# Three raw buffers for late weights, six for reads of h, reads five steps ahead and splits two, in a chain of attention and two feed-forward layers

## The chip, the cores and the metric

The kernel runs on one core of a Trainium2 chip. The metric is the time on the device in microseconds (us), lower is better; the time of a kernel is the median of several runs.

## The reference

Decay attention over 4 batches of 8 heads (576 positions, 64 wide) gives x, 2304 x 512. A feed-forward layer with Mish follows, then one with a maximum of three products. All arrays are float32.

```python
x = attention(q, k, v, f)                       # 2304 x 512
h = x @ moe_w_in                                # 2304 x 2048
g = h * np.tanh(np.log1p(np.exp(h)))            # Mish
y = g @ moe_w_out                               # 2304 x 512
m = np.maximum(np.maximum(y @ w1, y @ w2), y @ w3)   # 2304 x 768
out = m @ moe2_w_out                            # 2304 x 512
```

## The kernel before

Every product of two float32 arrays is made of three matmuls (`mm3`, L180 to L184): each operand is split into a high part and a low part (`split`, L135 to L143: the high part is a copy to the narrower type, L137 on ACT or L139 on POOL; the low part is the difference, L143 on DVE or POOL), and high by high, high by low and low by high are summed in PSUM.

Weights are read in chunks by `load_f32` (L147). A chunk comes in by a DMA of SP as raw 8-byte numbers (the tile r, named `wr` or `wr1`) and is made float32 in the tile `wt` by five operations of DVE: L160, L161, L164, L167 and L171. L160, L167 and L171 read the raw tile. `load_split` then splits `wt`, for the late weights both halves on POOL.

The work has three stages, which overlap at their edges:

1. Attention and h. PE makes x, and h from it in units of 256 tokens by 256 columns; a copy `he` (L542 on ACT, or on DVE) goes to DRAM, to `h_d`. Near its end `load_w_out` reads moe_w_out in 16 chunks of 128 x 512 (tiles `wo`), one for each unit of h. These use the raw tile `wr` with two buffers.
2. y, from about 490 to 717 us. 72 steps (`todo`) run over 5 blocks of tokens and 16 chunks of the 2048 columns: 64 steps with 512 tokens and 12 matmuls each, then 8 with 256 tokens and 24 matmuls. For a step, `load_g` reads h back from `h_d` (DMA on SP, L631), applies Mish on ACT (L634) and splits the result into gh (ACT, L137) and gl (DVE, L143). It is called three steps ahead of the matmuls, with tiles of four buffers each. At the end of a block four copies `ze` of y (tile pool `zst`, four buffers; two by ACT and two by DVE) go to DRAM, to `z_d`; the first 256 tokens of the first block come back at once and are split by ACT and POOL (`y0`).
3. The maximum of three products and the last product, 717 us to the end.

In stage 2 the weights of stage 3 are loaded too. `load_w2` has 24 chunks of 128 x 384 (tiles `wm`) and then 6 of 128 x 512 (`wo2`), and one chunk is asked for at every second step. These use a raw tile `wr1` of their own with one buffer: the DMA of a chunk cannot start before L171 of the chunk ahead has read it. The converted tile `wt` has two buffers in all of this.

Each engine does its instructions in the order of its own list. The lists come from a scheduler that simulates the program with costs of its own; priorities (`tc.high_priority(AHEAD)` around `load_g`) and buffers coming free in that simulation decide what is put first. So a change of buffer numbers moves instructions on all engines.

Of the kernel before, what the change touches and what calls it, by code (L numbers as in the profile page):

```python
# [9 lines left out]
F32 = mybir.dt.float32  # L10
F32R = mybir.dt.float32r
BF16 = mybir.dt.bfloat16
I32 = mybir.dt.int32
# [18 lines left out]
AHEAD = 3000  # L32
BLK = 256
BLK2 = 512
# [33 lines left out]
def tile_decay_attention__mish_ff__max3_ff(  # L68
# [66 lines left out]
    def split(dst_hi, dst_lo, src, eng_hi, eng_lo):  # L135
        if eng_hi == "act":
            nc.scalar.activation(dst_hi, src, AF.Copy)  # L137
        elif eng_hi == "pool":
            nc.gpsimd.tensor_scalar(dst_hi, src, 1.0, 1.0, op0=ALU.mult, op1=ALU.mult)  # L139
        else:  # L140
            nc.vector.tensor_copy(dst_hi, src)
        eng = nc.gpsimd if eng_lo == "pool" else nc.vector
        eng.tensor_tensor(out=dst_lo, in0=src, in1=dst_hi, op=ALU.subtract)  # L143
# [3 lines left out]
    def load_f32(pool, srcs, bufs=None, abs_eng="dve", raw="wr"):  # L147

        m, n = len(srcs), srcs[0].shape[1]
        t = pool.tile([128, m, n], F32, name="wt", tag="wt", bufs=bufs)  # L150
        r = pool.tile([128, m, n, 2], I32, name=raw, tag=raw, bufs=bufs if raw == "wr" else 1)

        with tc.issue_after(pace[-1].ins) if pace else ExitStack():
            for i, src in enumerate(srcs):
                nc.sync.dma_start(r[:, i].rearrange("p n w -> p (n w)"), src.bitcast(I32))
        lo, hi, ti = r[:, :, :, 0], r[:, :, :, 1], t.bitcast(I32)
        if abs_eng == "act":
            nc.scalar.activation(t, hi.bitcast(F32), AF.Abs)
        else:
            nc.vector.tensor_scalar(ti, hi, 0x7FFFFFFF, None, op0=ALU.bitwise_and)  # L160
        nc.vector.tensor_scalar(  # L161
            t, t, F32_MIN_AS_HIGH_HALF, F32_MAX_AS_HIGH_HALF, op0=ALU.max, op1=ALU.min
        )
        nc.vector.tensor_scalar(  # L164
            ti, ti, 3, 0x3FFFFFF8, op0=ALU.logical_shift_left, op1=ALU.bitwise_and
        )
        nc.vector.scalar_tensor_tensor(  # L167
            out=ti, in0=hi, scalar=-0x40000000, in1=ti,
            op0=ALU.bitwise_and, op1=ALU.bitwise_or,
        )  # L170
        nc.vector.scalar_tensor_tensor(  # L171
            out=ti, in0=lo, scalar=29, in1=ti,
            op0=ALU.logical_shift_right, op1=ALU.bitwise_or,
        )
        return t

    def load_split(pool, dst_hi, dst_lo, srcs, eng_hi, eng_lo, bufs=None, abs_eng="dve", raw="wr"):
        split(dst_hi, dst_lo, load_f32(pool, srcs, bufs, abs_eng, raw), eng_hi, eng_lo)

    def mm3(ps, whl, xhl, start, stop):  # L180
        (wh, wl), (xh, xl) = whl, xhl
        nc.tensor.matmul(ps, wh, xh, start=start, stop=False, skip_group_check=True)  # L182
        nc.tensor.matmul(ps, wh, xl, start=False, stop=False, skip_group_check=True)  # L183
        nc.tensor.matmul(ps, wl, xh, start=False, stop=stop, skip_group_check=True)  # L184
# [5 lines left out]
    wst = sa.enter_context(tc.tile_pool(name="wst", bufs=2))  # L190
# [39 lines left out]
    raw = [ap_.tile([128, 640 if c == "v" else S], F32, name=f"raw{c}") for c in "qkv"]  # L230
# [343 lines left out]
    sb = ExitStack()  # L574
# [1 line left out]
    wo = [wop.tile([128, 2, 2, DM], F32R, name=f"wo{fp}") for fp in range(NFP)]  # L576
    stg2 = sb.enter_context(tc.tile_pool(name="stg2", bufs=2, side="right", reuse_waits="tile"))
    gp_ = sb.enter_context(tc.tile_pool(name="gp", bufs=4, side="right", reuse_waits="tile"))
    zst = sb.enter_context(tc.tile_pool(name="zst", bufs=4, side="right", reuse_waits="tile"))
    yps = sb.enter_context(tc.tile_pool(name="yps", bufs=5, space=PSUM, side="right", reuse_waits="tile"))  # L580

    def load_w_out():
# [23 lines left out]
    def load_w2():  # L606
        for c in range(KD):
            for m in range(3):
                src = (moe2_w1, moe2_w2, moe2_w3)[m][c * 128:(c + 1) * 128, :]
                for d in range(0, DFF2, 384):  # L610
                    ds = slice(d, d + 384)
                    load_split(
                        stg2, wm[m][:, 0, c:c + 1, ds], wm[m][:, 1, c:c + 1, ds], [src[:, ds]],
                        "pool", "pool", raw="wr1",
                    )
                    yield
        for c in range(NF2):
            load_split(
                stg2, wo2[:, 0, c:c + 1, :], wo2[:, 1, c:c + 1, :],
                [moe2_w_out[c * 128:(c + 1) * 128, :]], "pool", "pool", raw="wr1",  # L620
            )
            yield

    def load_g(ib, fp, a):

        g = gp_.tile([128, BLK2], F32, name="g")
        gh = gp_.tile([128, BLK2], F32R, name="gh")
        gl = gp_.tile([128, BLK2], F32R, name="gl")
        n = blocks1[ib][1]
        if n == BLK2:  # L630
            nc.sync.dma_start(g, h_d[ib][fp][:, a, :])  # L631
        else:
            nc.sync.dma_start(g.rearrange("p (a n) -> p a n", a=2), h_d[ib][fp][:])
        nc.scalar.activation(g, g, AF.Mish)  # L634
        split(gh, gl, g, "act", "dve")
        return [(t, (gh[:, i * n:(i + 1) * n], gl[:, i * n:(i + 1) * n])) for i, t in enumerate([a] if n == BLK2 else [0, 1])]

    wgen3 = load_w2()
    todo = [(ib, fp, a) for ib, (_, n) in enumerate(blocks1) for fp in range(NFP) for a in range(n // BLK)]
    with tc.high_priority(AHEAD):  # L640
        ahead = [load_g(*t) for t in todo[:3]]
    for step, (ib, fp, a) in enumerate(todo):
        n = blocks1[ib][1]
        if fp == 0 and a == 0:
            y = [yps.tile([128, n], F32, name=f"y{j}", tag="y") for j in range(KD)]
        parts = ahead.pop(0)
        if step + 3 < len(todo):
            with tc.high_priority(AHEAD):
                ahead.append(load_g(*todo[step + 3]))
        for t, g in parts:  # L650
            final = fp == NFP - 1 and t == 1
            for j in range(KD):
                js = slice(j * 128, (j + 1) * 128)
                mm3(y[j], (wo[fp][:, 0, t, js], wo[fp][:, 1, t, js]), g, fp == 0 and t == 0, final)
        if step % 2:
            next(wgen3, None)
        if final:
            for j in range(KD):
                ze = zst.tile([128, n], F32, name="ze", tag="ze")
                if j % 2:  # L660
                    nc.vector.tensor_copy(ze, y[j])
                    nc.sync.dma_start(z_d[ib][:, j, :], ze)
                else:
                    nc.scalar.activation(ze, y[j], AF.Copy)
                    nc.scalar.dma_start(z_d[ib][:, j, :], ze)
            if ib == 0:
                nc.sync.dma_start(y0[0], z_d[0][:, :, 0:BLK])
                split(y0[1], y0[2], y0[0], "act", "pool")
# [12 lines left out]
    for t0, n in blocks2:  # L681
# [13 lines left out]
        for c2 in range(0, NF2, k2):  # L695
            gp = gps[c2 // k2 % 2]
            g = [gp.tile([128, k2, n], F32, name=f"g{m}") for m in range(3)]
# [52 lines left out]
```

## Time and profile before

| | us |
|---|---|
| median of 3 runs | 1026.43 (1024.89 to 1028.39) |
| profiled execution, its time | 1024.48 |
| its span in the trace | 1022.5 |
| PE busy | 955.2 (93%) |
| DVE busy | 511.9 (50%) |
| ACT busy | 422.0 (41%) |
| POOL busy | 378.3 (37%) |

The span is the profiled execution from its first instruction to its last; its own time has 2.0 us around that. PE is TensorE, DVE VectorE, ACT ScalarE, POOL GpSimd, SP the engine that issues most DMAs. "Busy" counts the time in which an engine has work, so it says nothing on which engine the others wait for; that is read from the waits.

### The profile page before, as it was taken

Reading aid. Unit: us, or ns where it says so; the run is one execution under the profiler, and the core shown is the slowest. Engines: PE = TensorE matmul, PEld = TensorE weight load, DVE = VectorE, ACT = ScalarE, POOL = GpSimd, SP = SyncE. Lnnn points to the kernel's source line nnn. Section 1 sums busy time; section 2 is a strip of 40 time slices with the busy share of each in tenths; the row PEclk is TensorE's granted clock in tenths of the full one; section 3 lists DMA queues with packets and bytes.
Section 4 is the critical chain, followed back from the end, with each engine's and each line's share of the span. In section 5 each row is a group of like instructions: output and inputs, shape, how many; then the busy total and the mean of one; then the engine's idle time right before and its main releaser. Section 6 shows DMA issues by size and latency. Waiting matters only on the chain.

```text
span 1022.5 us, 15879 instructions
## 1 busy us (share of the span) xinstructions
PE 955.2 (93%) x5756; PEld 840.6 (82%) x5756; DVE 511.9 (50%) x1159; ACT 422.0 (41%) x920; POOL 378.3 (37%) x437
## 2 busy tenths in 40 slices
PE   4886799999998999998898999999999999999998
PEld 4675689999998999998776777778988888888886
DVE  4868898656556556479645655653211112011110
ACT  4876667666667565421233434332211211211111
POOL 6756875566447521445423423230111111011110
PEclk9987789999999999999898999999999999999999
DMA  6545646545344412765445554552300100200101
GB/s 151 143 141 161 172 131 207 151 145 159 109 143 131 138 57 89 268 208 187 143 144 177 160 185 149 190 172 75 104 21 1 62 21 1 83 1 2 40 0 42
DMA packets 105294, 119.16 MB, mean 117 GB/s; under 512 B 33856, under 2 KB 77376, under 8 KB 105216
## 3 DMA queue, kind: packets, MB, share of 16 engines
q1 hardware_dynamic: 92288, 103.73, 33.0%
q10 hardware_dynamic: 12928, 14.42, 4.0%
q8 instruction: 45, 0.74, 0.3%
q14 instruction: 33, 0.27, 0.1%
HBM read 85.01 MB, written 33.10 MB: 116 GB/s over the span
## 4 chain that ended last, share of the span: by engine, by line
PE 57%; DMA 18%; DVE 17%; issue 2%; ACT 2%; SPq 2%; POOL 1%; DVEq 0%; ACTq 0%; POOLq 0%
PE g L183 7%; PE g L184 7%; PE g L182 7%; DMA wr<-in_moe_w_dram 7%; DMA wr<-in_moe_w_out_dram 5%; PE h L183 4%; PE h L184 4%; PE h L182 4%; PE av L451 4%; PE sc L363 4%; DVE wt L171 3%; PE pp L438 3%; DVE wt L167 3%; PE o L182 2%; PE o L184 2%; PE o L183 2%
## 5 line engine op out<-in xcount | busy, mean ns | idle before, releaser
L182 PE MATMUL h<-xh,wi 128*128 128x256 f32 x576 | 167.4, 292 | 8.2 <-ACT he L542 6.7
L183 PE MATMUL h<-xl,wi 128*128 128x256 f32 x576 | 167.1, 290 | 1.9 <-POOL xl L143 1.9
L184 PE MATMUL h<-xh,wi 128*128 128x256 f32 x576 | 166.2, 289 | 0.0
L143 POOL TENSOR_TENSOR hl<-mx,hh 128x512 fp32r<-128x512 f32 x27 | 36.5, 1350 | 271.3 <-ACT hh L137 271.3
L182 PE MATMUL g<-yh,wm 128*128 128x512 f32 (+1 forms) x360 | 134.5, 374 | 0.0
L183 PE MATMUL g<-yl,wm 128*128 128x512 f32 (+1 forms) x360 | 134.5, 374 | 0.0
L184 PE MATMUL g<-yh,wm 128*128 128x512 f32 (+1 forms) x360 | 134.5, 374 | 0.0
L183 PE MATMUL y<-gl,wo 128*128 128x512 f32 (+1 forms) x320 | 121.6, 380 | 10.5 <-DVE gl L143 10.5
L182 PE MATMUL y<-gh,wo 128*128 128x512 f32 (+1 forms) x320 | 120.5, 378 | 4.6 <-ACT gh L137 3.4
L182 PEld LDWEIGHTS h<-xh,wi 128*128 128x128 f32 x576 | 111.9, 195 | 9.5 <-ACT he L542 7.0
L184 PE MATMUL y<-gh,wo 128*128 128x512 f32 (+1 forms) x320 | 119.5, 375 | 0.0
L183 PEld LDWEIGHTS h<-xl,wi 128*128 128x128 f32 x576 | 111.9, 194 | 3.2 <-POOL xl L143 2.4
L184 PEld LDWEIGHTS h<-xh,wi 128*128 128x128 f32 x576 | 111.8, 194 | 0.3
L634 ACT ACTIVATE g<-g 128x512 f32<-128x512 f32 x72 | 45.5, 632 | 138.5 <-DMA g<-h_d 128.3
L706 DVE TENSOR_TENSOR mx<-g,mx 128x512 f32<-128x512 f32 x27 | 18.7, 691 | 158.6 <-PE g L184 158.6
L183 PEld LDWEIGHTS y<-gl,wo 128*128 128x128 f32 x320 | 61.8, 193 | 26.5 <-DVE gl L143 17.0
L414 ACT ACTIVATE P<-P,mn 128x128 f32<-128x128 f32 (+3 forms) x128 | 70.9, 556 | 27.3 <-DVE mn L408 26.4
L183 PEld LDWEIGHTS g<-yl,wm 128*128 128x128 f32 x360 | 68.2, 189 | 13.4
L184 PEld LDWEIGHTS g<-yh,wm 128*128 128x128 f32 x360 | 68.2, 189 | 13.2
L182 PEld LDWEIGHTS g<-yh,wm 128*128 128x128 f32 x360 | 68.1, 189 | 13.2
L182 PEld LDWEIGHTS y<-gh,wo 128*128 128x128 f32 x320 | 62.0, 194 | 17.3 <-ACT gh L137 4.9
L438 PE MATMUL pp<-ident,P 128*128 128x128 f32 x320 | 64.4, 303 | 11.9 <-POOL P L388 11.7
(101 smaller groups left out, 1989.9 us busy)
## 6 DMA issues: line engine op xcount, KB each, us to landing
g<-h_d SPq DMA_DIRECT2D x72, 256.0 KB, 3.3
h_d<-he ACTq DMA_DIRECT2D x46, 256.0 KB, 2.9
wr<-in_moe_w_out_dram SPq DMA_DIRECT2D x22, 512.0 KB, 4.0
wr<-in_moe_w_dram SPq DMA_DIRECT2D x24, 384.0 KB, 3.4
cb<-cum_d SPq DMA_DIRECT2D x64, 128.0 KB, 3.4
wr<-in_moe_w_in_dram SPq DMA_DIRECT2D x32, 256.0 KB, 3.3
h_d<-he SPq DMA_DIRECT2D x26, 256.0 KB, 3.2
cb<-cum_d SPq DMA_DIRECT2D x32, 144.0 KB, 3.3
```

The lines of the kernel that those rows point to most:

```text
L143: eng.tensor_tensor(out=dst_lo, in0=src, in1=dst_hi, op=ALU.subtract)
L167: nc.vector.scalar_tensor_tensor(out=ti, in0=hi, scalar=-0x40000000, in1=ti, op0=ALU.bitwise_and, op1=ALU.bitwise_or,)
L171: nc.vector.scalar_tensor_tensor(out=ti, in0=lo, scalar=29, in1=ti, op0=ALU.logical_shift_right, op1=ALU.bitwise_or,)
L182: nc.tensor.matmul(ps, wh, xh, start=start, stop=False, skip_group_check=True)
L183: nc.tensor.matmul(ps, wh, xl, start=False, stop=False, skip_group_check=True)
L184: nc.tensor.matmul(ps, wl, xh, start=False, stop=stop, skip_group_check=True)
L363: nc.tensor.matmul(o, lhs, rhs, start=n == 0, stop=n == len(mms) - 1, skip_group_check=True)
L414: nc.scalar.activation(Pt, Pt, AF.Exp, scale=-1.0, bias=mn[:, col - 1:col], accum_out=sm[:, ci:ci + 1],)
L438: nc.tensor.transpose(pp[:, n * 128:n * 128 + 128], Pt[:, k0:k0 + 128], ident)
L451: nc.tensor.matmul(avp[h][:, off:off + w], vl, T[:, i, c:c + w], start=kt == 0 and i == 0 and not (g == 0 and h == 1), stop=last and i == ...
L634: nc.scalar.activation(g, g, AF.Mish)
L706: nc.vector.tensor_tensor(out=mx, in0=g[1], in1=mx, op=ALU.max)
```

## The change

- All late weights share one raw tile `wr` with three buffers, where moe_w_out had two and the later ones one of their own. The room is the same.
- `load_g` only reads h and applies Mish, into tiles `g` with six buffers (before four), and is called five steps ahead (before three). A new function `split_g` makes gh and gl, with three buffers each (before four), and is called two steps ahead (before three). Six and two times three take the room of three times four.
- `zst` has three buffers, where it had four.

```diff
--- before.py
+++ after.py
@@ -148,7 +148,7 @@
 
         m, n = len(srcs), srcs[0].shape[1]
         t = pool.tile([128, m, n], F32, name="wt", tag="wt", bufs=bufs)
-        r = pool.tile([128, m, n, 2], I32, name=raw, tag=raw, bufs=bufs if raw == "wr" else 1)
+        r = pool.tile([128, m, n, 2], I32, name=raw, tag=raw, bufs=3 if pool is not wst else bufs)
 
         with tc.issue_after(pace[-1].ins) if pace else ExitStack():
             for i, src in enumerate(srcs):
@@ -576,7 +576,7 @@
     wo = [wop.tile([128, 2, 2, DM], F32R, name=f"wo{fp}") for fp in range(NFP)]
     stg2 = sb.enter_context(tc.tile_pool(name="stg2", bufs=2, side="right", reuse_waits="tile"))
     gp_ = sb.enter_context(tc.tile_pool(name="gp", bufs=4, side="right", reuse_waits="tile"))
-    zst = sb.enter_context(tc.tile_pool(name="zst", bufs=4, side="right", reuse_waits="tile"))
+    zst = sb.enter_context(tc.tile_pool(name="zst", bufs=3, side="right", reuse_waits="tile"))
     yps = sb.enter_context(tc.tile_pool(name="yps", bufs=5, space=PSUM, side="right", reuse_waits="tile"))
 
     def load_w_out():
@@ -611,42 +611,48 @@
                     ds = slice(d, d + 384)
                     load_split(
                         stg2, wm[m][:, 0, c:c + 1, ds], wm[m][:, 1, c:c + 1, ds], [src[:, ds]],
-                        "pool", "pool", raw="wr1",
+                        "pool", "pool",
                     )
                     yield
         for c in range(NF2):
             load_split(
                 stg2, wo2[:, 0, c:c + 1, :], wo2[:, 1, c:c + 1, :],
-                [moe2_w_out[c * 128:(c + 1) * 128, :]], "pool", "pool", raw="wr1",
+                [moe2_w_out[c * 128:(c + 1) * 128, :]], "pool", "pool",
             )
             yield
 
     def load_g(ib, fp, a):
 
-        g = gp_.tile([128, BLK2], F32, name="g")
-        gh = gp_.tile([128, BLK2], F32R, name="gh")
-        gl = gp_.tile([128, BLK2], F32R, name="gl")
+        g = gp_.tile([128, BLK2], F32, name="g", bufs=6)
         n = blocks1[ib][1]
         if n == BLK2:
             nc.sync.dma_start(g, h_d[ib][fp][:, a, :])
         else:
             nc.sync.dma_start(g.rearrange("p (a n) -> p a n", a=2), h_d[ib][fp][:])
         nc.scalar.activation(g, g, AF.Mish)
+        return g, n, [a] if n == BLK2 else [0, 1]
+
+    def split_g(g, n, tiles):
+        gh = gp_.tile([128, BLK2], F32R, name="gh", bufs=3)
+        gl = gp_.tile([128, BLK2], F32R, name="gl", bufs=3)
         split(gh, gl, g, "act", "dve")
-        return [(t, (gh[:, i * n:(i + 1) * n], gl[:, i * n:(i + 1) * n])) for i, t in enumerate([a] if n == BLK2 else [0, 1])]
+        return [(t, (gh[:, i * n:(i + 1) * n], gl[:, i * n:(i + 1) * n])) for i, t in enumerate(tiles)]
 
     wgen3 = load_w2()
     todo = [(ib, fp, a) for ib, (_, n) in enumerate(blocks1) for fp in range(NFP) for a in range(n // BLK)]
     with tc.high_priority(AHEAD):
-        ahead = [load_g(*t) for t in todo[:3]]
+        read = [load_g(*t) for t in todo[:5]]
+        ahead = [split_g(*read.pop(0)) for _ in range(2)]
     for step, (ib, fp, a) in enumerate(todo):
         n = blocks1[ib][1]
         if fp == 0 and a == 0:
             y = [yps.tile([128, n], F32, name=f"y{j}", tag="y") for j in range(KD)]
         parts = ahead.pop(0)
-        if step + 3 < len(todo):
-            with tc.high_priority(AHEAD):
-                ahead.append(load_g(*todo[step + 3]))
+        with tc.high_priority(AHEAD):
+            if step + 5 < len(todo):
+                read.append(load_g(*todo[step + 5]))
+            if read:
+                ahead.append(split_g(*read.pop(0)))
         for t, g in parts:
             final = fp == NFP - 1 and t == 1
             for j in range(KD):
```

How the lists of the engines differ, at two places. First DVE, where the chunks of 384 columns are converted beside the steps of y (`wt` is the converted chunk, `wr1` or `wr` the raw one, gl the low part of a step's input). Before:

```order
L160 TENSOR_SCALAR wt_7032<-wr1_7033 128x384
L161 TENSOR_SCALAR wt_7032<-wt_7032 128x384
L164 TENSOR_SCALAR wt_7032<-wt_7032 128x384
L143 TENSOR_TENSOR gl_7015<-g_7013,gh_7014 128x512
L167 SCALAR_TENSOR_TENSOR wt_7032<-wr1_7033,wt_7032 128x384
L171 SCALAR_TENSOR_TENSOR wt_7032<-wr1_7033,wt_7032 128x384
L143 TENSOR_TENSOR gl_7044<-g_7042,gh_7043 128x512
L160 TENSOR_SCALAR wt_7080<-wr1_7081 128x384
L161 TENSOR_SCALAR wt_7080<-wt_7080 128x384
```

With the change:

```order
L160 TENSOR_SCALAR wt_7130<-wr_7131 128x384
L171 SCALAR_TENSOR_TENSOR wt_7082<-wr_7083,wt_7082 128x384
L161 TENSOR_SCALAR wt_7130<-wt_7130 128x384
L164 TENSOR_SCALAR wt_7130<-wt_7130 128x384
L143 TENSOR_TENSOR gl_7019<-g_6948,gh_7018 128x512
L167 SCALAR_TENSOR_TENSOR wt_7130<-wr_7131,wt_7130 128x384
L160 TENSOR_SCALAR wt_7178<-wr_7179 128x384
L171 SCALAR_TENSOR_TENSOR wt_7130<-wr_7131,wt_7130 128x384
L161 TENSOR_SCALAR wt_7178<-wt_7178 128x384
L164 TENSOR_SCALAR wt_7178<-wt_7178 128x384
L143 TENSOR_TENSOR gl_7048<-g_6967,gh_7047 128x512
L167 SCALAR_TENSOR_TENSOR wt_7178<-wr_7179,wt_7178 128x384
```

Before, a chunk's five operations and two gl alternate; with the change there is one gl to a chunk, L160 of the next chunk stands ahead of L171 of the one before it, and L164 is followed at once by a gl.

Second, ACT at the end of h (`he` is the copy of h, its DMA goes to `h_d`; `g` on itself is Mish; gh the high part). Before:

```order
L542 ACTIVATE he_6594<-h_6569 128x512
L545 DMA h_d2048_3_104<-he_6594 128x512
L634 ACTIVATE g_6946<-g_6946 128x512
L542 ACTIVATE he_6632<-h_6607 128x512
L545 DMA h_d2048_4_105<-he_6632 128x512
L542 ACTIVATE he_6670<-h_6645 128x512
L545 DMA h_d2048_5_106<-he_6670 128x512
L542 ACTIVATE he_6708<-h_6683 128x512
L545 DMA h_d2048_6_107<-he_6708 128x512
L542 ACTIVATE he_6746<-h_6721 128x512
L545 DMA h_d2048_7_108<-he_6746 128x512
L137 ACTIVATE gh_6870<-g_6869 128x512
```

With the change:

```order
L542 ACTIVATE he_6594<-h_6569 128x512
L545 DMA h_d2048_3_104<-he_6594 128x512
L542 ACTIVATE he_6632<-h_6607 128x512
L545 DMA h_d2048_4_105<-he_6632 128x512
L542 ACTIVATE he_6670<-h_6645 128x512
L545 DMA h_d2048_5_106<-he_6670 128x512
L542 ACTIVATE he_6708<-h_6683 128x512
L137 ACTIVATE gh_6874<-g_6804 128x512
L545 DMA h_d2048_6_107<-he_6708 128x512
L542 ACTIVATE he_6746<-h_6721 128x512
L545 DMA h_d2048_7_108<-he_6746 128x512
L632 ACTIVATE g_6948<-g_6948 128x512
```

The Mish of g_6946 stood ahead of the last four copies of h; the one that answers to it now, g_6948, stands behind the last of them.

## Rows read from the trace of the kernel before

**Rows 1.** The page, part 1: engines over the whole span.
```profile
PE 955.2 (93%) x5756; PEld 840.6 (82%) x5756; DVE 511.9 (50%) x1159; ACT 422.0 (41%) x920; POOL 378.3 (37%) x437
```

**Rows 2.** Busy time by stretch: us from:to, length, each engine, clock, DMA share, GB/s.
```profile
440.00:497.00 57.00, 50.25 (x386) 49.35 (x385) 49.77 (x66) 10.64 (x18) 29.07 (x27) 0.94 0.57 190
497.00:717.00 220.00, 204.83 (x951) 166.78 (x950) 119.07 (x227) 80.02 (x140) 64.19 (x63) 0.97 0.47 153
```

**Rows 3.** Groups of PE by form, 497 to 717 us: busy, mean ns, idle before.
```profile
L183 PE MATMUL y<-gl,wo 128*128 128x512 f32 x247 | 99.3, 402 | 8.3 <-DVE gl L143 8.3
L182 PE MATMUL y<-gh,wo 128*128 128x512 f32 x246 | 97.8, 399 | 3.6 <-ACT gh L137 3.1 <-DVE ze L661 0.5
```

**Rows 4.** Timeline of PE: ten 512-wide starts, then ten 256-wide ones.
```profile
599.54 0.39 PE L183 MATMUL y<-gl,wo 128*128 128x512 f32 x1
...
601.80 0.39 PE L184 MATMUL y<-gh,wo 128*128 128x512 f32 x1
...
707.79 0.28 PE L184 MATMUL y<-gh,wo 128*128 128x256 f32 x1
...
709.00 0.28 PE L182 MATMUL y<-gh,wo 128*128 128x256 f32 x1
```

**Rows 5.** Waits of DVE, 440 to 717 us: us in total, times, longest.
```profile
DVE wt L160 <- DMA wr<-in_moe_w_dram: 57.0, 22, 4.1
...
DVE wt L160 <- POOL wo L143: 2.0, 1, 2.0
```

**Rows 6.** Timeline of DVE: one late chunk of 384 columns and the next one's start.
```profile
510.51 0.36 DVE L160 TENSOR_SCALAR wt<-wr 128x384 int32<-128x384 int32 x1 [3.10 <-DMA wr<-in_moe_w_dram]
...
513.24 0.68 DVE L143 TENSOR_TENSOR gl<-g,gh 128x512 fp32r<-128x512 f32 x1
517.21 0.36 DVE L160 TENSOR_SCALAR wt<-wr 128x384 int32<-128x384 int32 x1 [3.29 <-DMA wr<-in_moe_w_dram]
```

**Rows 7.** Timeline of DVE: one late chunk of 512 columns.
```profile
661.48 0.43 DVE L160 TENSOR_SCALAR wt<-wr 128x512 int32<-128x512 int32 x1 [0.61 <-DMA wr<-in_moe_w_out_dram]
...
663.48 0.69 DVE L143 TENSOR_TENSOR gl<-g,gh 128x512 fp32r<-128x512 f32 x1
664.08 0.69 DVE L171 SCALAR_TENSOR_TENSOR wt<-wr,wt 128x512 int32<-128x512 int32 x1
```

**Rows 8.** Timeline of DVE during the chunks of moe_w_out.
```profile
430.58 1.67 DVE L171 SCALAR_TENSOR_TENSOR wt<-wr,wt 128x512 int32<-128x512 int32 x1
...
464.47 0.51 DVE L160 TENSOR_SCALAR wt<-wr 128x512 int32<-128x512 int32 x1 [0.48 <-DMA wr<-in_moe_w_out_dram]
...
473.45 1.40 DVE L164 TENSOR_SCALAR wt<-wt 128x512 int32<-128x512 int32 x1
...
476.47 0.81 DVE L160 TENSOR_SCALAR wt<-wr 128x512 int32<-128x512 int32 x1 [0.18 <-DMA wr<-in_moe_w_out_dram]
...
489.46 0.54 DVE L160 TENSOR_SCALAR wt<-wr 128x512 int32<-128x512 int32 x1 [0.44 <-DMA wr<-in_moe_w_out_dram]
...
493.85 0.47 DVE L160 TENSOR_SCALAR wt<-wr 128x512 int32<-128x512 int32 x1 [0.51 <-DMA wr<-in_moe_w_out_dram]
```

**Rows 9.** Timeline of POOL: splits of x, of wo, and one of wm.
```profile
439.55 2.72 POOL L143 TENSOR_TENSOR xl<-xr,xh 128x1024 fp32r<-128x1024 f32 x1
...
472.40 0.73 POOL L139 TENSOR_SCALAR wo<-wt 128x512 fp32r<-128x512 f32 x1 [1.82 <-DVE wt L171]
473.21 1.34 POOL L143 TENSOR_TENSOR wo<-wt,wo 128x512 fp32r<-128x512 f32 x1
...
501.70 1.02 POOL L143 TENSOR_TENSOR wm<-wt,wm 128x384 fp32r<-128x384 f32 x1
```

**Rows 10.** Timeline of PE, then of ACT, at the long stall.
```profile
488.45 0.58 PE L182 MATMUL h<-xh,wi 128*128 128x256 f32 x1 [6.75 <-ACT he L542]
...
487.29 0.63 ACT L634 ACTIVATE g<-g 128x512 f32<-128x512 f32 x1 [11.14 <-DMA g<-h_d]
```

**Rows 11.** The page, part 6: reads of h, KB each, us to landing.
```profile
g<-h_d SPq DMA_DIRECT2D x72, 256.0 KB, 3.3
```

## Prediction

> **What bounds the kernel now.** I began with the page's share of busy time [rows 1]: PE 93%, DVE 50%. That says that only TensorE can be worth much, and not where. So next came busy time by stretch [rows 2]. In the stretch 497 to 717 us, where y is made, PE is busy 204.8 of 220 us at a granted clock of 0.97, the higher of its two levels; DVE works 119.1 us and the DMAs carry 153 GB/s at a share of 0.47. Everything after 717 us is the third stage, which the change touches only at its start.
>
> Busy time hides some loss, because pipelined matmuls overlap. The pitch is the better measure [rows 4]: ten 512-wide matmuls start in 601.80 − 599.54 = 2.26 us, so 0.227 us each and 12 × 0.227 = 2.72 us for a step; ten 256-wide ones take 1.22 us, 0.121 us each. The stretch holds some 740 of the first kind (247 and 246 in the forms of [rows 3], and as many of the third product), 192 of the second, and 12 of stage 3: 168 + 23.2 + 1.5 = 193. So PE loses **about 27 us** of 220. What it waits for is gl on DVE, 8.3 us, and gh on ACT, 3.1 us [rows 3]; the rest are stretched starts around these waits.
>
> Why gl is late is seen in DVE's waits [rows 5]: 22 times L160, the first operation of a late chunk, stood for its raw DMA, 57.0 us in all, and every gl behind it stood too. One such chunk is shown whole [rows 6]: L160 waits 3.10 us, the chunk's first three operations and a gl follow, then the next L160 waits 3.29 us. With one raw buffer the transfer cannot start before the last conversion of the chunk ahead has read it. Before the stretch there is one more loss: PE stands 6.75 us for ACT's copy of h, because ACT's Mish ahead of it waited 11.14 us for its read [rows 10]. The most the change can give is 27 + 6.75 = **34 us**.
>
> **What the change does, by part.** *Three raw buffers.* Raw DMAs are issued two chunks earlier, so the 57.0 us of waits should go. But what follows is not an idle DVE. The order (shown above) puts a chunk to **each** gl where there was one to two. All 30 chunks then end by the gl of step 38, where before they ran to step 68; after it 33 gl stand alone. The work isn't smaller, it is moved forward and packed.
>
> *What a packed chunk costs.* Alone, a 384 chunk with a gl takes 513.24 − 510.51 = 2.73 us [rows 6], which is just PE's step of 2.72. A 512 chunk with a gl takes 664.08 + 0.69 − 661.48 = 3.29 us, with the gl 0.60 of it (664.08 − 663.48) [rows 7]; so 2.13 and 2.69 without a gl. Packed, POOL's splits of the chunk ahead lie on it. The trace shows that for the 16 chunks of moe_w_out [rows 8]: L164 takes 1.40 us at 473.45 where POOL's L143 ran 1.34 us from 473.21 [rows 9]. Between 464.47 and 493.85 seven chunks and one gl ran, so (29.38 − 0.60 − 0.18 − 0.44 − 0.51) / 7 = 3.95 us per chunk. Thus POOL's work adds 3.95 − 2.69 = 1.26 us. For 384 columns I scale it by POOL's own durations, 1.02 / 1.34 [rows 9]: 0.96. A packed cycle is then 2.73 + 0.96 = **3.69 us** (384) or 3.29 + 1.26 = **4.55 us** (512), against PE's 2.72. DVE becomes the bound of the first half. The bounds are 0 (POOL's halves fall beside operations that they don't hold) and POOL's whole time, 0.73 + 1.34 = 2.07 for 512 columns and by the same scale 1.53 for 384. I take the measured 1.26 because in the new order, too, a chunk's first operations follow the last of the chunk ahead.
>
> *The clock of DVE.* A chunk of moe_w_out ends at 430.58 + 1.67 = 432.25 [rows 8]. By the order 14 of these chunks, two of 384 and two gl come before the gl of step 5: 14 × 3.95 = 55.3, 2 × 3.09 = 6.2, 2 × 0.60 = 1.2, POOL's split of x in the way 2.7 [rows 9], one wait for POOL to free a converted buffer 2.0 [rows 5]. Sum: 499.7 us. From there to step 38: 22 × 3.69 = 81.2, 6 × 4.55 = 27.3, six gl without chunk 3.6, four copies of y at a gl's 0.69 [rows 7] 2.8, the split of y's first block on POOL 2.7, and for two block ends with three zst buffers where there were four 2 × 1 us (between nothing and 3.3 each, the landing of a 256 KB transfer [rows 11]; I take the low part, since ACT and DVE share the copies). Sum: **619.3 us**. Then PE is the bound: 26 × 2.72 = 70.7, eight steps of 24 × 0.121 = 23.2, two block ends 1.6, and 18 matmuls of stage 3 that the order now puts in between, 2.2. y ends at **717.0 us**, where it ended before. What was won in the second half was spent in the first.
>
> *The stall of 6.75 us* goes, since the order puts that Mish behind the last copy of h. It is worth nothing: PE finishes h earlier, and then waits for gl of step 5 at 499.7.
>
> *Six buffers for reads, splits two ahead.* Reads leave five steps ahead, some 5 × 2.72 = 13.6 us, against a landing of 3.3 us [rows 11]; they are not late by themselves. ACT's load doesn't change (80 of 220 us [rows 2]), so I cost it at nothing, under PE's and DVE's cover; without that cover it is the third rival.
>
> *Order of PE.* 33 matmuls of stage 3 stand before the last y where 12 stood. In the first half they fill waits: (33 − 12) × 0.121 = 2.5 us off the end.
>
> **Sum.** 1024.48 − 2.5 = 1022.0 us for an execution like the profiled one. That lies 1.95 below the median of the three runs, 1026.43, so I forecast **1024 us** at the median's level. The term that decides is the exposure to POOL: 44 packed chunks, so 0.1 us in each moves the end 4.4 us. With 0.2 us either way this case spans 1015 to 1033.
>
> **Rivals.** *Fast: PE stays the bound.* If POOL's halves fall into the gl or into the two-operand conversions without holding them, a cycle stays near 2.73 and the 34 us are won: 1026.43 − 34 = 992; at half the exposure, near 1004. For it: alone, the 384 cycle equals PE's step [rows 6]. Against it: the seven packed chunks in a row of [rows 8]. Chance 0.20.
>
> *Slower: POOL holds DVE for its whole time.* In the new order, L171 is followed by L161 and L164, so POOL's first half lies on L161 and its second on L164. If both are held in full, a 512 chunk costs 0.81 more (2.07 − 1.26) and a 384 one 0.57 more: 20 × 0.81 + 24 × 0.57 = 30 us, so 1054; at half of that 1039. It decides from an exposure above 1.3 us per 384 chunk. Against it: the 1.26 already includes whatever the first half of the split cost there. Chance 0.14. The Trainium skill, "SBUF — State Buffer", section "Who interferes with whom", says that VectorE and GpSimd share one port pair as an exclusive lock, and that the one that comes second blocks for the whole instruction. By that rule the row of 1.40 us beside 1.34 us [rows 8, 9] is what is to be expected, and packing chunks onto splits gives away in lock time what it wins in DMA waits. By the rule at its full strength the time would be the 1054 above.
>
> *Slower: the read loop.* Only three gh and gl buffers, and ACT, in order, does Mish of a later read ahead of gh. The loop from a gl to the next but one is then landing 3.3 [rows 11], Mish 0.63 [rows 10], gh about the same, gl 0.69: 5.3 us for two steps that last 5.44. It decides where reads land after more than 3.3 us. At 0.5 us more, each step of the last 26 takes 0.25 longer: +6.5 us, 1030; at twice that, 1037. For it: nothing but the thin margin; against it: six buffers put the read itself further ahead. Chance 0.10.
>
> *The raw reads stay late*, so that the waits only change their owner: near the old time, 1026. Against it: the DMAs were used at 0.57 even where two buffers served, at 190 GB/s [rows 2], and a 384 chunk every 3.69 us is less. Chance 0.06.
>
> **Numbers.** My forecast has 0.50. About 0.3%, 3.1 us, can be told from no change; 1024 lies inside, and its spread gives 0.20 faster, 0.22 the same, 0.08 slower. With the fast rival (0.20 faster), POOL's (0.14 slower), the read loop (0.08 slower, 0.02 the same) and the late reads (0.04 the same, 0.02 faster): **0.42 faster, 0.28 the same, 0.30 slower**. The range 1005 to 1040 holds the forecast, half-strength forms of the first two rivals, and the read loop; the full 992 and 1054 lie outside.
>
> **What would show it.** Right: L160's waits for raw DMA fall from 57 us to a few; DVE is busy over 85% from 440 to near 620 us, with L161 or L164 stretched past 1 us beside POOL; PE waits for gl at most steps until then and runs at 2.72 us a step after; the last chunk ends near step 38; ACT's long wait for a read ahead of h is gone. Wrong: cycles of 384 chunks near 2.7 us with PE gapless from 500 on (fast); gaps of PE after 620 that end on gh or gl with ACT waiting for g (read loop); an interval between L160s above 4.2 us (POOL in full).

## The result, and the profile after

| | before | after |
|---|---|---|
| median, us | 1026.04 (4 runs) | 1015.25 (4 runs) |
| profiled execution, us | 1024.48 | 1014.82 |
| its span | 1022.5 | 1012.7 |

The ratio is 0.9875 (95% interval 0.9851 to 0.9898): faster by 1.25%. The two medians alone give 0.9895, inside that interval. The forecast was 1024, within what can't be told from no change, so its one number missed the gain, though faster had the largest chance, 0.42. The measured time lies inside the range, at the fast edge of what I gave the forecast's own case, 1015 to 1033.

First the page of the changed kernel, busy time of the engines, which answers to [rows 1]:

```profile
PE 946.9 (94%) x5756; PEld 830.2 (82%) x5756; DVE 533.9 (53%) x1159; ACT 423.4 (42%) x920; POOL 373.7 (37%) x437
```

DVE has 22 us more of busy time with the same 1159 instructions. Busy time by stretch shows where (from:to, length, PE, PEld, DVE, ACT, POOL, granted clock, DMA share, GB/s); the stretch from 497 us is cut where the late loads now end:

```profile
440.00:497.00 57.00, 55.04 (x421) 52.81 (x419) 53.70 (x73) 11.75 (x21) 30.65 (x29) 1.00 0.65 206
497.00:612.00 115.00, 100.75 (x404) 75.21 (x405) 108.12 (x179) 40.66 (x70) 54.87 (x58) 0.97 0.61 193
612.00:717.00 105.00, 105.00 (x593) 92.49 (x592) 28.42 (x43) 41.34 (x70) 2.29 (x2) 1.00 0.34 108
```

From 497 to 612 us DVE is busy 94% of the time and PE has gaps; after 612 PE has none. That is the two halves of the forecast: DVE bounds the first, PE the second. The waits of DVE from 440 to 717 us (us in total, times, longest) show that the 57.0 us of [rows 5] are gone; L160 now waits for POOL alone, 2.9 us:

```profile
DVE gl L143 <- ACT gh L137: 67.0, 33, 4.5
DVE ze L667 <- PE y L184: 6.6, 1, 6.6
DVE ze L667 <- DMA z_d<-ze: 3.1, 4, 1.5
...
DVE wt L160 <- POOL wo L143: 2.0, 1, 2.0
DVE wt L160 <- POOL wm L143: 0.9, 1, 0.9
```

A second line of the same view of the kernel before went with them, which the prediction did not count; 15.7 us of it are waits of the six chunks of 512 columns after 654 us:

```profile
DVE wt L160 <- DMA wr<-in_moe_w_out_dram: 18.8, 12, 4.5
```

And PE, by form, 497 to 717 us, which answers to [rows 3]: its waits for gl rose from 8.3 to 14.7 us, while those for gh nearly went:

```profile
L183 PE MATMUL y<-gl,wo 128*128 128x512 f32 x236 | 95.8, 406 | 14.7 <-DVE gl L143 14.7
...
L182 PE MATMUL y<-gh,wo 128*128 128x512 f32 x235 | 81.9, 395 | 0.7 <-DVE ze L667 0.4 <-ACT gh L137 0.3
```

What a packed cycle is made of can be read in DVE's timeline (start, length, operation), one chunk of 384 columns and one gl, in the steady part:

```profile
520.21 0.55 DVE L164 TENSOR_SCALAR wt<-wt 128x384 int32<-128x384 int32 x1
520.68 1.51 DVE L143 TENSOR_TENSOR gl<-g,gh 128x512 fp32r<-128x512 f32 x1
522.12 0.54 DVE L167 SCALAR_TENSOR_TENSOR wt<-wr,wt 128x384 int32<-128x384 int32 x1
522.59 0.35 DVE L160 TENSOR_SCALAR wt<-wr 128x384 int32<-128x384 int32 x1
522.86 0.55 DVE L171 SCALAR_TENSOR_TENSOR wt<-wr,wt 128x384 int32<-128x384 int32 x1
523.33 0.34 DVE L161 TENSOR_SCALAR wt<-wt 128x384 f32<-128x384 f32 x1
523.71 0.55 DVE L164 TENSOR_SCALAR wt<-wt 128x384 int32<-128x384 int32 x1
524.18 1.51 DVE L143 TENSOR_TENSOR gl<-g,gh 128x512 fp32r<-128x512 f32 x1
```

and beside it POOL's timeline in the same kernel:

```profile
519.99 0.55 POOL L139 TENSOR_SCALAR wm<-wt 128x384 fp32r<-128x384 f32 x1 [1.84 <-DVE wt L171]
520.63 1.02 POOL L143 TENSOR_TENSOR wm<-wt,wm 128x384 fp32r<-128x384 f32 x1
```

The cycle is 524.18 − 520.68 = **3.50 us**, against PE's 2.72. The gl that starts 0.05 us after POOL's low half takes 1.51 us, where it is 0.69 alone [rows 6]: it is held nearly until POOL is done at 521.65, and does its work then.

### The profile page after: what moved, and what is told of

It reads as the page before. It is cut to its first block, busy times and chain, and to the rows that moved or that the text cites. A ratio compares the mean times of both kernels' runs of the same rounds, so it can differ in the third digit from the quotient of the medians.

```text
span 1012.7 us, 15919 instructions
## 1 busy us (share of the span) xinstructions
PE 946.9 (94%) x5756; PEld 830.2 (82%) x5756; DVE 533.9 (53%) x1159; ACT 423.4 (42%) x920; POOL 373.7 (37%) x437
## 4 chain that ended last, share of the span: by engine, by line
PE 62%; DVE 19%; DMA 8%; issue 5%; ACT 2%; POOL 2%; SPq 1%; ACTq 0%; DVEq 0%; POOLq 0%
PE g L182 7%; PE g L183 7%; PE g L184 7%; PE av L451 4%; PE h L183 4%; PE h L184 4%; PE h L182 4%; PE sc L363 3%; DVE wt L164 3%; PE y L183 3%; DVE wt L167 3%; PE y L184 3%; PE y L182 3%; PE pp L438 3%; PE o L182 3%
## 5 line engine op out<-in xcount | busy, mean ns | idle before, releaser
L182 PE MATMUL h<-xh,wi 128*128 128x256 f32 x576 | 165.3, 288 | 2.2 <-DVE he L539 1.4
L184 PE MATMUL h<-xh,wi 128*128 128x256 f32 x576 | 164.2, 286 | 0.0
L183 PE MATMUL y<-gl,wo 128*128 128x512 f32 (+1 forms) x320 | 121.7, 380 | 14.7 <-DVE gl L143 14.7
L184 PE MATMUL y<-gh,wo 128*128 128x512 f32 (+1 forms) x320 | 118.6, 374 | 0.0
L182 PEld LDWEIGHTS h<-xh,wi 128*128 128x128 f32 x576 | 109.8, 191 | 3.7 <-DVE he L539 1.7
L184 PEld LDWEIGHTS h<-xh,wi 128*128 128x128 f32 x576 | 109.9, 191 | 0.3
L182 PE MATMUL y<-gh,wo 128*128 128x512 f32 (+1 forms) x320 | 108.2, 373 | 0.7 <-DVE ze L667 0.4
L143 DVE TENSOR_TENSOR gl<-g,gh 128x512 fp32r<-128x512 f32 x72 | 63.6, 885 | 71.4 <-ACT gh L137 71.4
```

## The experiments

Each kernel is compared with the kernel before on the same chip; times of different groups of runs are compared by their ratios.

| run | edit | median, us | ratio (95% interval) |
|---|---|---|---|
| change | all | 1015.25 | 0.9875 (0.9851 to 0.9898) |
| 1 | raw buffers alone | 1009.68 | 0.9846 (0.9824 to 0.9867) |
| 2 | reads and splits alone | 1029.99 | 1.0037 (1.0017 to 1.0057) |
| 3 | change, no POOL in late splits | 991.60 | 0.9671 (0.9644 to 0.9699) |
| 4 | change, raw DMAs spaced | 1021.10 | 0.9961 (0.9940 to 0.9982) |
| 5 | change, Mish behind gh | 1012.00 | 0.9845 (0.9817 to 0.9873) |
| 6 | run 1, chunks spaced on DVE | 1003.53 | 0.9766 (0.9730 to 0.9802) |
| 7 | run 1, no POOL | 993.85 | 0.9666 (0.9631 to 0.9701) |
| 8 | runs 6 and 7 together | 992.16 | 0.9653 (0.9623 to 0.9683) |
| 9 | run 5, chunks spaced on DVE | 988.62 | 0.9628 (0.9600 to 0.9656) |
| 10 | change, zst four | 1013.83 | 0.9876 (0.9851 to 0.9901) |
| 11 | run 9, no POOL | 986.78 | 0.9609 (0.9584 to 0.9634) |
| 12 | run 9, two raw buffers | 993.54 | 0.9680 (0.9645 to 0.9716) |

**Which part carries it: runs 1, 2 and 10.** Run 1 is the kernel before with only

```diff
-        r = pool.tile([128, m, n, 2], I32, name=raw, tag=raw, bufs=bufs if raw == "wr" else 1)
+        r = pool.tile([128, m, n, 2], I32, name=raw, tag=raw, bufs=3 if pool is not wst else bufs)
...
-                        "pool", "pool", raw="wr1",
+                        "pool", "pool",
```

(and the same for `wo2`); run 2 is the change without these lines and with zst four.

> Only the three raw buffers; the reads of h stay three steps ahead with four buffers, zst keeps four. Theory A (the waits of the late chunks for their raw DMA were the loss; what replaces them is DVE converting one chunk per gl with POOL's splits on top): the order of DVE is nearly that of the change, so DVE's waits of L160 for a DMA fall from 57 us to under 5, the last chunk ends near 612 us and the time is 1012 to 1020 us. Theory B (the gain comes from the reads further ahead and the removed stall of 6.75 us before 490 us): 1022 to 1028 us, at most 4 us better than before.

> Only the reads five steps ahead and the splits two; raw buffers two and one and zst four as before. Theory A: L160 still waits some 55 us for raw DMAs, in cycles of one chunk to two gl, so y ends within 3 us of before; the stall of 6.75 us before 490 us is gone, which is hidden behind the gl that wait for moe_w_out's chunks: 1021 to 1029 us. Theory B: 1012 to 1020 us.

The raw buffers carry all of it. Alone they gain 1.5% (the time is 2 us below the range of theory A), the reads alone lose 0.4%. In run 2 the waits of L160, 440 to 717 us, are still there:

```profile
DVE wt L160 <- DMA wr<-in_moe_w_dram: 68.5, 22, 4.0
```

Run 2 came out slower than I expected; PE's waits for gl from 497 to 717 us are 22.1 us there against 8.3 [rows 3], which fits splits that are only two steps ahead of a DVE that stalls for 3 us at a time; that link was not tried by itself. Run 1 also shows that the stall of 6.75 us [rows 10] could stay (5.3 us in it) without harm, since gl was later than h.

Run 10, `zst` with four buffers in the change:

> The change with four buffers for the copies of y in place of three. Theory: in the half that DVE bounds, each wait of DVE's copy for a store to land is on the path; the change shows 3.1 us of them in four waits. They go, y ends some 3 us earlier and the time is 1010 to 1014 us. Rival (the waits are covered by gl that are ahead): 1014 to 1017.

The 3.1 us of waits for a store went, the end of y moved by 0.9 us, and the ratio is that of the change to 0.0001, each with an interval of some 0.0025 to either side. The fourth zst buffer is worth nothing that can be measured. The time of 1013.83 us lies in the range of the theory only because the kernel before took 1027.37 in that group of runs.

**Is it POOL that holds DVE: runs 3 and 7.** In both, the late weights' halves are made by ACT and DVE:

```diff
-                        "pool", "pool",
+                        "act", "dve",
```

> The change, with the late weights' high parts made by ACT and low parts by DVE in place of both by POOL. Theory A (DVE is held by POOL's splits: gl takes 1.51 us beside POOL's 1.02, alone 0.69): DVE gets 0.47 us of own work per 384 chunk (0.60 per 512) and loses 0.76 (1.17) of being held, so a 384 cycle falls from 3.49 to about 3.2 us, gl stays near 0.69 us everywhere, and the time falls by 10 to 17 us below the change, to 998 to 1006. Rival C (the long operations of DVE have nothing to do with POOL's): the added work comes on top, cycles near 3.95 us, and the time rises by 10 us, to about 1025.

> Only the three raw buffers, and the late weights' halves made by ACT and DVE. Theory A: no long gl, as in the run with the full change and no POOL (991.6 us). If the reads further ahead cost 5 us here too: 984 to 988. If that loss was only the late gl of step 6, which does not occur without POOL's splits: 989 to 994.

Groups of DVE by form, 497 to 612 us (busy, mean ns, idle before), first of the change, then of run 3:

```profile
L143 DVE TENSOR_TENSOR gl<-g,gh 128x512 fp32r<-128x512 f32 x34 | 35.9, 1058 | 4.5 <-ACT gh L137 4.5
```

```profile
L143 DVE TENSOR_TENSOR gl<-g,gh 128x512 fp32r<-128x512 f32 x39 | 26.8, 687 | 10.3 <-ACT gh L137 10.3
L143 DVE TENSOR_TENSOR wm<-wt,wm 128x384 fp32r<-128x384 f32 x22 | 13.4, 615 | 4.9 <-ACT wm L137 4.9
```

The same gl is 1058 ns with POOL's splits beside it and 687 without. DVE was given more instructions and got through its list sooner: by the ratios 0.0204 of 1026, 21 us off the change. That shows the hold, and refutes the rival by which long operations had another cause. It gained more than I expected (998 to 1006). One reason is in the order: the 16 chunks of moe_w_out also became cheaper, and gl of step 5 came at 468 us where it was 497. Run 7 is like run 3 (0.9666 and 0.9671): without POOL's splits the reads further ahead make no difference that these intervals can show.

The Trainium skill, "SBUF — State Buffer", section "Who interferes with whom", says that a VectorE instruction with two inputs in SBUF contends with a GpSimd instruction that reads SBUF, and that whichever comes second waits for the whole of the other. gl has two such inputs and started 0.05 us second; its 1.51 us agree with that rule to 0.15 us: what was left of POOL's operation, 0.97 us, and gl's own 0.69 would be 1.66.

**Is it the packing: runs 4, 6, 8 and 9.** If one chunk to a gl is too much for DVE, one chunk to two gl is not. Run 4 spaced the raw DMAs, each behind the newest read of h on SP:

```diff
-            nc.sync.dma_start(g, h_d[ib][fp][:, a, :])
+            pace[:] = [nc.sync.dma_start(g, h_d[ib][fp][:, a, :])]
```

> The change, with each late chunk's raw DMA queued on SP behind the newest read of h, so that DVE's order has one chunk to two gl until step 60 in place of one to one until step 38. Theory A (one chunk per gl at 3.49 us against PE's step of 2.72 is what bounds the first half of y): two gl and one chunk cost 2 x 0.60 + 2.13 + 0.76 = 4.1 us against 5.44 us of PE, so PE runs from 500 us with at most a few us of waits, y ends near 688 us where it ended at 709, and the time is 990 to 1000 us. Rival D (DVE isn't what holds PE; reads of h are): the time stays within 4 us of the change, 1011 to 1019.

This failed. In DVE's timeline and then SP's, a chunk in run 4:

```profile
521.04 0.36 DVE L160 TENSOR_SCALAR wt<-wr 128x384 int32<-128x384 int32 x1 [2.71 <-DMA wr<-in_moe_w_dram]
```

```profile
517.29 0.32 SPq L629 DMA_DIRECT2D g<-h_d  x1
517.66 0.43 SPq L155 DMA_DIRECT2D wr<-in_moe_w_dram  x1
518.37 4.78 SPq L629 DMA_DIRECT2D g<-h_d  x2
```

SP held the raw DMA back until the read ahead of it had a free buffer (from 497 to 612 us SP's reads of h waited 76.2 us for gl to free one). It issued the raw DMA at 517.66 us, 3.4 us before L160 could start and only 0.7 us before L160 stood waiting. The three buffers did not help: L160 waited 63.2 us for the weights of w1 to w3 from 440 to 717 us, more than before. Neither theory had this; the wait I had put back was the one that the change took away. So the next runs left the DMAs free and spaced DVE's work, L160 behind the newest gl (`behind` holds it; the lines of L160 to L171 move down by two):

```diff
-            nc.vector.tensor_scalar(ti, hi, 0x7FFFFFFF, None, op0=ALU.bitwise_and)
+            with tc.issue_after(behind[-1].ins) if behind else ExitStack():
+                nc.vector.tensor_scalar(ti, hi, 0x7FFFFFFF, None, op0=ALU.bitwise_and)
```

> Only the three raw buffers, with the reads as before, and DVE's first operation on each late chunk queued behind the newest gl, so that chunks come one to two gl while their raw DMAs are free to go three chunks ahead (in the run that paced the DMAs themselves, these came late, and L160 waited 63 us for them). Theory A (DVE at one chunk per gl is the bound of the first half): L160 waits under 15 us for DMAs in all, PE loses under 6 us from 500 us on, y ends near 683 us and the time is 985 to 995 us. Rival D (spaced chunks meet late raw reads however they are spaced): over 40 us of such waits, 1005 us or more.

> The two edits of the last two kernels together: three raw buffers, chunks spaced on DVE, halves by ACT and DVE. Both take away the same loss in the stretch from 497 us, so by theory A the sum is little better than the better of them: PE is gapless from 440 us to the end of y but for 3 us, and the time is 983 to 990 us. If the two added up, it would be under 975.

> The full change, with DVE's first operation on each late chunk queued behind the newest gl (one chunk to two gl) and Mish of the later read behind gh. POOL still makes the halves. Theory A: 2 x 0.60 + 2.13 + 0.76 = 4.1 us of DVE for two steps of 5.44 us on PE, so PE is the bound as soon as step 5 has its gl at 498 us: 59 steps x 2.72 + 23.2 + some 5 us of block ends and stage 3 give an end of y at 687 us where the change has 709, and 990 to 998 us. Raw buffers alone with the same spacing ended y at 691, because PE came to 497 us three steps behind. Rival D (waits for late raw reads come back): over 40 us of them, and 1005 us or more.

In run 9 the theory holds, and a little more was won than it gave: 988.6 us against 990 to 998, with the end of y at 681 us against 687. Its busy time by stretch:

```profile
432.00:497.00 65.00, 64.95 (x479) 61.51 (x478) 61.56 (x83) 16.79 (x29) 35.95 (x33) 1.00 0.66 212
497.00:612.00 115.00, 115.00 (x513) 95.41 (x514) 86.65 (x155) 51.94 (x91) 45.79 (x46) 1.00 0.62 199
612.00:717.00 105.00, 105.00 (x649) 94.73 (x649) 46.84 (x69) 35.03 (x57) 20.66 (x17) 1.00 0.36 113
```

PE has 513 matmuls in the stretch where the change has 404, no gap, and the clock at its higher level throughout; L162 (L160 before) never waits for a raw DMA; DVE is busy 75% of it, though POOL's splits still hold it (L162, 0.36 us alone, has a mean of 0.60 there). Run 6 had no waits for raw DMAs either, but missed its 985 to 995 us: y ended at 691 in the profiled execution, its fastest (999.33 us). Its profile shows the likely reason, in the stretch before:

```profile
432.00:497.00 65.00, 59.76 (x454) 58.11 (x453) 59.58 (x78) 14.58 (x26) 36.41 (x35) 0.95 0.65 209
```

PE stood 5.2 us for the copy of h there, the stall of [rows 10], and entered the stretch behind run 9. What was hidden under the late gl is on the path once gl is early: the reads five steps ahead, which cost 0.4% alone, are now part of the gain, together with the Mish put behind gh (run 6 has neither, and the two were not tried apart in the spaced kernel). Run 8 shows that spacing and freeing DVE from POOL do not add: 0.9653, against 0.9766 and 0.9666 for the two by themselves. Its 992 us are a little over what I expected, 983 to 990.

**The rest of the distance between the change and run 1: run 5.** In the change, ACT's timeline shows gh of steps 6 and 7 behind a Mish whose read SP had issued behind five raw DMAs:

```profile
501.13 0.63 ACT L632 ACTIVATE g<-g 128x512 f32<-128x512 f32 x1 [10.30 <-DMA g<-h_d]
501.67 1.14 ACT L137 ACTIVATE gh<-g 128x512 fp32r<-128x512 f32 x2
```

Run 5 makes `split_g` come before `load_g` in a step and queues Mish behind the newest gh (`hi`):

```diff
-        nc.scalar.activation(g, g, AF.Mish)
+        with tc.issue_after(hi[-1].ins) if hi else ExitStack():
+            nc.scalar.activation(g, g, AF.Mish)
```

> The change, with ACT's Mish of the read five steps ahead queued behind the gh of the split two ahead. In the change gh of step 6 stood from 490 to 501 us behind the Mish of step 11, whose read SP issued behind five raw reads of the next weights, and gl of step 6 came at 502.3 us; with the raw buffers alone it came at 497.2. Theory A (that one place is the 5 to 6 us by which the full change is behind the raw buffers alone): gl of step 6 by 498 us and 1008 to 1012 us. Rival (the loss is spread over all steps, by three gh and gl buffers in place of four): 1013 to 1017 us.

gl of step 6 came by 499 us where it had come at 502.3, and y ended 2.0 us earlier. The ratio is that of run 1, but its interval overlaps that of the change, so this is shown by the profile only, and for 2 us of the 5 to 6 that the theory gave. Part of what lies between the change and run 1 stays open.

**How far it goes: runs 11 and 12.**

> The kernel of the spaced run, with the late halves by ACT and DVE. Once spaced, POOL's hold on DVE costs PE nothing after 500 us; what is left to win is before that, where 16 packed chunks decide when step 5 gets its gl: PE gapless from 440 to the end of y at 683 to 687 us, 986 to 992 us.

> The kernel of 988.6 us (spaced on DVE, Mish behind gh, halves by POOL) with two raw buffers in place of three. Theory: at one chunk in 5.44 us two buffers give a read of 3.5 us time enough, L160 waits under 15 us in all for raw reads, gl of step 5 comes by 500 us and the time is 986 to 994 us. Rival: with two buffers the reads of moe_w_out are late as before the change, step 5 has its gl only near 504 us, and the time is 995 us or more.

Run 11 is within the interval of run 9, and y ends at 681 us in both: once DVE has time to spare, being held by POOL costs PE nothing. There was nothing left to win before 497 us, as PE was already busy 56.95 of the 57 us from 440 in run 9. Run 12 needs the third raw buffer before 497 us, where chunks of moe_w_out are still packed. There, from 432 to 497 us, the waits are

```profile
DVE wt L162 <- DMA wr<-in_moe_w_out_dram: 6.1, 5, 2.0
```

and PE then loses 4.8 us in one wait for gl; after that, two buffers at one chunk to two gl keep L162 from waiting. The measured time, 993.5, lies in the range of the theory, at the end next to the rival's, and part of the rival is true.

## Why the prediction was right, and where it was off

**The mechanism** came out as forecast: raw waits gone, DVE the bound until the loads end, PE without gaps after; the last chunk at the gl of step 38. The size did not: the load stretch was priced too high, and by that the gain was missed.

**The clock of DVE**, against the trace of the change:

```profile
497.16 0.69 DVE L143 TENSOR_TENSOR gl<-g,gh 128x512 fp32r<-128x512 f32 x1
...
611.95 0.68 DVE L143 TENSOR_TENSOR gl<-g,gh 128x512 fp32r<-128x512 f32 x1
```

Step 5 had its gl at 497.2 us (forecast 499.7), step 38 at 612.0 (forecast 619.3). From there the last product of y took 709.3 − 612.0 = 97.4 us (forecast 717.0 − 619.3 = 97.7):

```profile
709.22 0.28 PE L184 MATMUL y<-gh,wo 128*128 128x256 f32 x1
709.33 0.28 PE L182 MATMUL g<-yh,wm 128*128 128x256 f32 x1
```

What follows y is 1012.7 − 709.3 = 303.4 us, where it was some 306 before: the 2.5 us of stage 3's matmuls done early are there. So the whole error, 7.3 us of the span, is in the load stretch.

**The term that failed** is not the hold, which I had called the one that decides. From the timeline above, POOL costs a 384 cycle 0.47 − 0.27 = 0.20 us on L164 (its step of 0.47 to the next start, where an operation of that form takes 0.27 to the next at 522.59) and 1.44 − 0.60 = 0.84 on gl: 1.04 us, forecast 0.96. What was too high is "alone, a 384 chunk with a gl takes 2.73 us": without the hold the cycle is 3.50 − 1.04 = 2.46. In [rows 6] a chunk's operations mostly stand one behind the other, each needing the last one's output. Three of them, from the kernel before:

```profile
510.90 0.36 DVE L161 TENSOR_SCALAR wt<-wt 128x384 f32<-128x384 f32 x1
...
512.18 0.55 DVE L167 SCALAR_TENSOR_TENSOR wt<-wr,wt 128x384 int32<-128x384 int32 x1
512.76 0.56 DVE L171 SCALAR_TENSOR_TENSOR wt<-wr,wt 128x384 int32<-128x384 int32 x1
```

L160 to L161 takes 0.39 us there, L167 to L171 0.58. In the new order, L160 of the next chunk stands between L167 and L171, and the steps after the same two forms are 0.27 us (from 522.59) and 0.47 (from 522.12). I had this order in front of me and read only what POOL meets in it. On balance the cycle shown took 3.50 us where 3.69 was forecast, which over 22 chunks would be 4.2 us.

By stretch the 7.3 us fall as these lines of the change's DVE give them:

```profile
464.32 0.42 DVE L160 TENSOR_SCALAR wt<-wr 128x512 int32<-128x512 int32 x1
...
472.03 0.42 DVE L160 TENSOR_SCALAR wt<-wr 128x512 int32<-128x512 int32 x1
...
502.31 0.69 DVE L143 TENSOR_TENSOR gl<-g,gh 128x512 fp32r<-128x512 f32 x1 [4.47 <-ACT gh L137]
...
544.36 0.69 DVE L667 COPY ze<-y 128x512 f32<-128x512 f32 x1 [0.17 <-DMA z_d<-ze]
...
584.64 0.41 DVE L160 TENSOR_SCALAR wt<-wr 128x512 int32<-128x512 int32 x1
...
611.34 0.69 DVE L171 SCALAR_TENSOR_TENSOR wt<-wr,wt 128x512 int32<-128x512 int32 x1
```

- Step 5 had its gl 2.5 us early. Two packed chunks of moe_w_out, from 464.32 to 472.03 us, took 3.86 each (forecast 3.95); 14 like these give 1.3 us, and the other 1.2 us are open.
- From 497.16 to 584.64, with the 22 chunks of 384 columns, it is 87.5 us where 619.3 − 499.7 − 29.3 = 90.3 was forecast: 2.8 us.
- The six of wo2, with seven gl and two copies of y, took 27.4 us from 584.64 to 612.03 (forecast 6 x 4.55 + 0.60 + 2 x 0.69 = 29.3): 1.9 us.

So the middle stretch gave less than the 4.2 us of its cycles. The late gl of step 6, a wait of 4.5 us that I had put at nothing (under "DVE's cover"), is in it, and against that stand the 2 us for zst, of which DVE stood 0.17 us in the load stretch, and smaller terms that I have not separated. That the forecast was off by no more than 7.3 us is in part luck: without that late gl the error would have been larger, by 2.0 us if run 5 is the measure, which took that wait away, and by 4.5 at most.

**Which operation is held** I had wrong for the steady 384 columns: gl, not L161 and L164. In later chunks, where the order differs, it is L161, L164 or L167 after all, for 1.07 to 1.27 us. For 512 columns of moe_w_out it is L164 and L167, as the changed kernel's DVE shows:

```profile
473.24 1.39 DVE L164 TENSOR_SCALAR wt<-wt 128x512 int32<-128x512 int32 x1
...
477.43 1.66 DVE L167 SCALAR_TENSOR_TENSOR wt<-wr,wt 128x512 int32<-128x512 int32 x1
...
571.38 1.07 DVE L164 TENSOR_SCALAR wt<-wt 128x384 int32<-128x384 int32 x1
```

**The rivals.** The fast one (PE stays the bound) did not happen, but the 34 us that it named were really there: run 9 ends 37.8 us of span earlier than before. POOL in full did not happen: the low half's 1.02 us cost DVE 0.84, but L139's 0.55 us only 0.20, because L164 started 0.22 us after it (520.21 and 519.99 above). What counts is what is left of POOL's operation when DVE's next one starts. The read loop shows in one place, steps 6 and 7, for a few us, and not at every step. The raw reads were not late. The range was said to hold the fast rival at half the exposure, but 1004 lies 1 us outside 1005 to 1040.

## What to carry to other kernels

A wait that is removed from an engine which is also short of time turns into that engine's own work: before counting the wait as gain, lay out its new order and price a cycle of it, with what other engines hold and with the latency between dependent operations that interleaving takes out. More buffers let a scheduler pull work forward; if the work has no hurry, space it on the engine that is short, and leave its DMAs free to run ahead. A stall that is hidden costs nothing until the cover goes, so parts of a change that lose alone can win together.

## What the runs showed of the hardware that was not expected

Which operation of DVE is held changes with the order of the list, and so does what the hold costs. L164, with one int32 input in SBUF, took 1.39 us beside POOL's low half (473.24 above), as [rows 8] had shown, and 0.43 with no split of POOL beside it:

```profile
426.65 0.43 DVE L164 TENSOR_SCALAR wt<-wt 128x512 int32<-128x512 int32 x1
```

In the steady chunks of 384 columns it stands ahead of POOL's low half and takes 0.55 us, and gl takes the hold.

TensorE's clock fell after a short stall. PE had waited 2.0 us for gl of step 5 in the change (until 497.90 us); the granted clock was then 0.52 from 500.0 to 502.4 us, near the lower of the two levels, and matmuls started 0.43 us apart in place of 0.227:

```profile
499.36 0.63 PE L182 MATMUL y<-gh,wo 128*128 128x512 f32 x1
499.79 0.63 PE L183 MATMUL y<-gl,wo 128*128 128x512 f32 x1
500.21 0.63 PE L184 MATMUL y<-gh,wo 128*128 128x512 f32 x1
```

It cost nothing here, since PE then still stood 0.30 us for gh of step 6. That the stall was the cause was not tried by itself.
